# A GEGLU feed-forward kernel: ScalarE's activation table is loaded behind the last weights of the first pair

## The chip, the cores and the metric

The kernel runs on one core of a Trainium2 chip. The core has five engines with an instruction queue each: TensorE (PE, matrix products into the PSUM memory), VectorE (DVE), ScalarE (ACT), GpSimd (POOL) and SyncE (SP). Sixteen DMA engines move data between HBM and the on-chip memory SBUF. In this kernel DMAs are issued from SP's queue and from ScalarE's queue. The metric is the device time of one execution in microseconds (us); the median of several runs is compared.

## What is computed

```python
def _gelu(x):
    return jax.nn.gelu(x, approximate=True)

# x: [1, 2048, 1024], w_gate and w_up: [1024, 3584], w_down: [3584, 1024], all bfloat16
def reference(x, w_gate, w_up, w_down):
    return (_gelu(x @ w_gate) * (x @ w_up)) @ w_down
```

## The kernel before

The 2048 tokens are worked on in two halves of 1024, each half as two blocks of 512 tokens (`tb` 0 and 1). The 1024 inner rows of x and of the weights are cut into eight slices of 128 (`kd` 0 to 7; `KH` is 4, `KD` is 8). The 3584 columns of `w_gate` and `w_up` are loaded in chunks of 512, and a chunk holds two pairs of 128-column blocks. Each half first makes h = gelu(gate) * up for 14 pairs, then the product with `w_down`. Nearly all of this uses seven products in place of eight for a 2x2 scheme of blocks (Strassen's way): sums of weight blocks, called s1, s2, s3, s4 and a22, and sums of x blocks, called t1 to t4 and b22, are made beforehand by POOL, VectorE and ScalarE, and TensorE multiplies these sums in fp32r. `pair_quads` does that for a pair; its products are m1, m5, m6, m2, m7, m3 and m4. In m5 the sum s1 is used, in m6 s2.

Only the first pair of the first half is done with plain products (`first_pair_units`), since its sums could not be ready. TensorE starts with seven matmuls on constants (`warm`, L201-L211). For token block 0 the slices 0 to 3 of x come as rows (`load_x0`, two loads for the first half of the columns and one for the second) and TensorE turns them (`transpose_x0`); VectorE and, for slice 3, ScalarE (L311) copy the result from PSUM. The slices 4 to 7 and all of token block 1 are turned by DMA transposes on SP's queue (`load_xT`, L168-L175). While the first pair is multiplied, POOL makes s1, s2 and s4 of the second pair from columns 256 to 511 of the first chunk (`s_sum`, L378), and VectorE makes s3 and the t sums.

The order of the instructions on each engine is written out by hand: the helpers `sp`, `act`, `dve`, `pool` and `pe` tie each instruction to the one before it on its engine. What stands on the queues at the start is:

- ScalarE: x columns 0-255, second half of the rows (L188); x columns 256-511 (L190); gate slices 2-4 of the first 256 columns (L192); the activation table (L194); gate slices 5-7 and up slices 5-7 of the same columns (L217-L219); then the copy of L311 and the gelus.
- SP: x columns 0-255, first half of the rows; gate slices 0-1; up slices 0-1; up slices 2-4 (L187-L193); four transposes for slices 4 to 7 of token block 0 (L216); three for token block 1, of 2, 2 and 4 slices (L221); gate and up of columns 256-511 (L223); chunk 1 of gate and up, whole (L226).

Between the engines, the program's planner places the DMAs of both queues in one list, gives each a completion semaphore out of eight in turn, and lets a DMA wait until the one that used its semaphore before has landed in full. Where two queues meet in this list is worked out by the planner and is not written in the code. The instruction records of the trace show each DMA's semaphore and what it waits for.

```python
    load_w(first, 1, 2, 5, sp, 0, FA)
    act(nc.scalar.preload_act_table(ACT.Gelu_apprx_tanh))
...
    for kd in range(KH, KD):
        load_xT(xT, 0, 0, kd, kd + 1)
        if kd == KH + 1:
            for j in range(2):
                load_w(first, j, 5, KD, act, 0, FA)
```

Of the kernel before, what the change touches and what calls it, by code (L numbers as in the profile page):

```python
# [8 lines left out]
ACT = mybir.ActivationFunctionType  # L9
# [25 lines left out]
def kernel(  # L35
# [8 lines left out]
    nc = tc.nc  # L44
# [65 lines left out]
    def on(engine, inst):  # L110

        if engine in last_on:
            tc.add_manual_dep(
                inst.ins, last_on[engine].ins.name, SCHED_DEP, reason="engine order"
            )
        last_on[engine] = inst
        return inst
# [4 lines left out]
    def act(inst):  # L122
        return on("act", inst)
# [31 lines left out]
    def load_w(key, j, k0, k1, queue=sp, f0=0, f1=FG):  # L155

        c0 = key[1] * FG
        eng = nc.scalar if queue is act else nc.sync
        src = (wgv, wuv)[j][:, k0:k1, c0 + f0 : c0 + f1]
        queue(eng.dma_start(out=chunks[key][j][:, k0:k1, f0:f1], in_=src))  # L160
# [7 lines left out]
    def load_xT(xT, h, tb, k0, k1):  # L168
        t0 = h * SH + tb * TB
        sp(  # L170
            nc.sync.dma_start_transpose(
                out=xT[tb][:, k0:k1, :],
                in_=xv[t0 : t0 + TB, k0:k1, :],
            )
        )  # L175
# [15 lines left out]
    load_w(first, 1, 0, 2, sp, 0, FA)  # L191
    load_w(first, 0, 2, 5, act, 0, FA)  # L192
    load_w(first, 1, 2, 5, sp, 0, FA)  # L193
    act(nc.scalar.preload_act_table(ACT.Gelu_apprx_tanh))  # L194
    ident = const_pool.tile([P, P], BF16, name="ident")
    make_identity(nc, ident[:])

# [17 lines left out]
    for kd in range(KH, KD):  # L215
        load_xT(xT, 0, 0, kd, kd + 1)  # L216
        if kd == KH + 1:  # L217
            for j in range(2):
                load_w(first, j, 5, KD, act, 0, FA)  # L219
    for k0, k1 in ((0, 2), (2, KH), (KH, KD)):  # L220
        load_xT(xT, 0, 1, k0, k1)  # L221
    for j in range(2):
# [779 lines left out]
```

## Time and profile before

| | us |
|---|---|
| median of 7 runs | 539.99 (539.79 to 540.49) |
| the profiled execution | 540.73 |
| its span, first to last instruction | 538.7 |
| TensorE matmuls busy | 532.8 |
| VectorE, ScalarE, POOL busy | 363.5, 263.2, 244.6 |
| table load on ScalarE (L194) | 1.283, from 2.35 to 3.63 |

The profile is of one execution. Its page gives the busy time of each engine and its share of the span; then the span in 40 equal slices, each digit the busy tenths of a slice, with the clock that was granted to TensorE (PEclk); the DMA queues; the chain of work that ended last, followed back from the end; and the costliest groups of instructions. A timeline line has the start, the duration, the engine, the line of the code, the operation, what is written and read, how many instructions were merged, and in brackets how long the engine sat idle ahead of it and what ended that. "PEld" is TensorE's weight load, "ACTq" and "SPq" are the issuing of DMAs by ScalarE and SyncE. Names such as `w_mem` (weights), `s_mem` (the s sums), `t_mem` (the t sums) and `bank` (PSUM) are those of the code. A busy share of the DMA engines over 1 means that packets of one engine overlap. Some records of matmuls are missing in a trace, which shows as a gap of exactly one matmul.

### The profile page before, as it was taken

The page shows a single profiled execution, that of the slowest core. Times are in us where ns is not written, and L with a number is a line of the kernel's source. Part 1 is how long each engine was busy: PE and PEld are TensorE (multiplying, and loading weights), DVE is VectorE, ACT ScalarE, POOL GpSimd, SP SyncE. Part 2 cuts the span into 40 slices and gives each one's busy share as a digit, 9 for nine tenths or more (in the row PEclk, how much of TensorE's full clock was granted, in tenths as well). Part 3 has the DMA queues.
Part 4 walks back from the last instruction along what each step waited for, and adds up shares of the span by engine and source line. Part 5 has one row for each costly group of instructions (what it writes and reads, how often), then busy time and mean ns, then how long its engine had stood idle before and what let it go on. Part 6 is the DMA issues. An engine that isn't in the chain of part 4 may idle for free.

```text
span 538.7 us, 7067 instructions
## 1 busy us (share of the span) xinstructions
PE 532.8 (99%) x2348; PEld 378.1 (70%) x2384; DVE 363.5 (67%) x475; ACT 263.2 (49%) x446; POOL 244.6 (45%) x212
## 2 busy tenths in 40 slices
PE   9999999999999999999999999999999999999997
PEld 4577777766776676777776777777777766866866
DVE  1988776788775997889574334444444469969961
ACT  1655555555555319217465555555555551452270
POOL 0699877777776000000056776666777730000000
PEclk9999999999999999999999999999999999999999
DMA  9936776697815977789950404042222448677846
GB/s 207 318 127 199 196 262 191 213 241 237 289 63 196 359 244 244 240 271 306 329 174 1 156 1 158 16 141 66 91 78 80 157 137 284 226 242 243 293 144 208
DMA packets 92435, 102.70 MB, mean 191 GB/s; under 512 B 18672, under 2 KB 67312, under 8 KB 92400
## 3 DMA queue, kind: packets, MB, share of 16 engines
q1 hardware_dynamic: 69600, 80.30, 47.0%
q10 hardware_dynamic: 22800, 21.96, 13.1%
q8 instruction: 19, 0.31, 0.3%
q14 instruction: 16, 0.13, 0.1%
HBM read 85.98 MB, written 12.58 MB: 183 GB/s over the span
## 4 chain that ended last, share of the span: by engine, by line
PE 99%; issue 0%; ACT 0%; ACTq 0%
PE bank L406 63%; PE bank L693 33%; PE bank L257 3%; PE bank L203 1%; PE bank L301 0%; ACT o_sb L746 0%; ACT bank L461 0%; ACTq L746 0%; ACTq L461 0%
## 5 line engine op out<-in xcount | busy, mean ns | idle before, releaser
L406 PE MATMUL bank<-t_mem,s_mem 128*128 128x512 f32 x1056 | 249.6, 394 | 0.0
L406 PEld LDWEIGHTS bank<-t_mem,s_mem 128*128 128x128 f32 x1056 | 198.1, 188 | 44.1 <-DVE bank L429 0.4
L378 POOL TENSOR_TENSOR s_mem<-w_mem 128x512 fp32r<-128x512 bf16 x102 | 120.7, 1205 | 190.8 <-DMA out_dram<-o_sb 103.1
L693 PE MATMUL bank<-t_mem,s_mem 128*128 128x512 f32 x544 | 127.1, 392 | 0.0
L281 DVE TENSOR_TENSOR hT<-w_mem,bank 128x512 bf16<-128x512 f32 x104 | 71.2, 686 | 80.5 <-PE bank L406 46.2
L693 PEld LDWEIGHTS bank<-t_mem,s_mem 128*128 128x128 f32 x544 | 102.2, 188 | 22.1
L429 DVE TENSOR_TENSOR bank<-bank,m 128x512 f32<-128x512 f32 x108 | 69.9, 694 | 44.4 <-ACT m L451 43.3
L406 PE MATMUL bank<-xT,w_mem 128*128 128x512 bf16 x405 | 96.5, 380 | 1.4
L276 ACT ACTIVATE w_mem<-bank 128x512 f32<-128x512 f32 x104 | 61.8, 596 | 53.4 <-DVE bank L429 35.8
L406 PEld LDWEIGHTS <-w_mem 128*128 128x128 bf16 x432 | 40.2, 98 | 51.6 <-issue 6.8
L378 POOL TENSOR_TENSOR s_mem<-w_mem,s_mem 128x512 fp32r<-128x512 bf16 x52 | 65.9, 1293 | 0.0
L598 DVE TENSOR_TENSOR t_mem<-w_mem 128x1024 fp32r<-128x1024 bf16 x56 | 65.5, 1216 | 0.0
L378 POOL TENSOR_TENSOR s_mem<-s_mem,w_mem 128x512 fp32r<-128x512 f32 x52 | 60.7, 1189 | 0.0
L457 ACT COPY bank<-bank 128x512 f32<-128x512 f32 x54 | 30.8, 570 | 38.9 <-PE bank L406 38.9
L391 ACT CAST s_mem<-w_mem 128x512 fp32r<-128x512 bf16 x54 | 33.1, 615 | 30.6 <-PE bank L406 28.0
L668 DVE TENSOR_TENSOR s_mem<-hT 128x512 fp32r<-128x512 bf16 x52 | 34.2, 684 | 10.0 <-PE bank L693 9.4
L451 ACT COPY m<-bank 128x512 f32<-128x512 f32 x54 | 31.7, 587 | 17.5 <-PE bank L406 17.5
L693 PEld LDWEIGHTS <-hT 128*128 128x128 bf16 x224 | 21.3, 98 | 26.6 <-issue 2.1
L461 ACT COPY bank<-bank 128x512 f32<-128x512 f32 x54 | 30.7, 570 | 12.7 <-PE bank L406 12.7
L746 ACT CAST o_sb<-bank 128x512 bf16<-128x512 f32 x28 | 15.4, 586 | 39.6 <-PE bank L693 39.6
L623 DVE TENSOR_TENSOR o_sb<-wd_sb,o_sb 128x512 fp32r<-128x512 bf16 x28 | 31.5, 1125 | 0.5
L595 ACT CAST t_mem<-w_mem 128x1024 fp32r<-128x1024 bf16 x28 | 26.9, 1048 | 0.0
(42 smaller groups left out, 238.3 us busy)
## 6 DMA issues: line engine op xcount, KB each, us to landing
t_mem<-t_dram SPq DMA_DIRECT2D x56, 512.0 KB, 5.2
w_mem<-in_w_gate_dram ACTq DMA_DIRECT2D x10, 1024.0 KB, 5.2
w_mem<-in_w_up_dram ACTq DMA_DIRECT2D x10, 1024.0 KB, 5.4
wd_sb<-in_w_down_dram SPq DMA_DIRECT2D x28, 256.0 KB, 4.2
t_dram<-o_sb SPq DMA_DIRECT2D x28, 256.0 KB, 2.8
wd_sb<-in_w_down_dram SPq DMA_DIRECT2D x12, 512.0 KB, 7.8
w_mem<-in_w_down_dram SPq DMA_DIRECT2D x4, 1024.0 KB, 6.3
w_mem<-in_w_down_dram SPq DMA_DIRECT2D x8, 512.0 KB, 8.6
```

The source lines that it names most:

```text
L276: act(nc.scalar.activation(out=g_sb, in_=ps[:], func=ACT.Gelu_apprx_tanh))
L281: nc.vector.tensor_tensor(out=hT[:, fc, tb * TB : (tb + 1) * TB], in0=g_sb, in1=ps[:], op=ALU.mult,)
L378: pool(nc.gpsimd.tensor_tensor(out=t, in0=in0, in1=in1, op=op))
L391: act(nc.scalar.copy(out=t, in_=a(1, 1)))
L406: nc.tensor.matmul(banks[bank][:], lhsT=lhs[:, c, :], rhs=rhs[:, c, :], start=start and c == 0, stop=c == KH - 1, skip_group_check=True,)
L429: nc.vector.tensor_tensor(out=banks[dst][:], in0=banks[src][:], in1=m5[j][:], op=ALU.add)
L451: act(nc.scalar.copy(out=m5[j][:], in_=banks[V_[j]][:]))
L457: act(nc.scalar.copy(out=banks[RB[j]][:], in_=banks[QB[j]][:]))
L598: dve(nc.vector.tensor_tensor(out=t, in0=in0, in1=in1, op=ALU.subtract))
L623: dve(nc.vector.tensor_tensor(out=t, in0=in0, in1=in1, op=ALU.subtract))
L668: dve(nc.vector.tensor_tensor(out=t, in0=in0, in1=in1, op=op))
L693: nc.tensor.matmul(banks[bset[u]][:], lhsT=lhs(i, u), rhs=rhs(i), start=start and i == 0, stop=stop and i == NS - 1, skip_group_check=True,)
```

## The change

The load of the activation table is moved on ScalarE's queue from its place ahead of the weight slices 5 to 7 to the place behind them. No other line is changed.

```diff
@@ -191,7 +191,6 @@
     load_w(first, 1, 0, 2, sp, 0, FA)
     load_w(first, 0, 2, 5, act, 0, FA)
     load_w(first, 1, 2, 5, sp, 0, FA)
-    act(nc.scalar.preload_act_table(ACT.Gelu_apprx_tanh))
     ident = const_pool.tile([P, P], BF16, name="ident")
     make_identity(nc, ident[:])
 
@@ -217,6 +216,7 @@
         if kd == KH + 1:
             for j in range(2):
                 load_w(first, j, 5, KD, act, 0, FA)
+            act(nc.scalar.preload_act_table(ACT.Gelu_apprx_tanh))
     for k0, k1 in ((0, 2), (2, KH), (KH, KD)):
         load_xT(xT, 0, 1, k0, k1)
     for j in range(2):
```

## The prediction

> **What bounds the kernel now.** I read the page first (busy shares, slices, chain of waits), then the timeline of the first 27 us, then busy times by stretch. From the page:
>
> ```profile
> PE 532.8 (99%) x2348; PEld 378.1 (70%) x2384; DVE 363.5 (67%) x475; ACT 263.2 (49%) x446; POOL 244.6 (45%) x212
> PEclk9999999999999999999999999999999999999999
> PE 99%; issue 0%; ACT 0%; ACTq 0%
> ```
>
> TensorE is busy from 0.77 us to 535.5 us and is nearly the whole chain. A change can only save what TensorE stands still for, or make it stand still. Matmuls of 512 columns start 0.427 us apart up to about 6.5 us and 0.216 us apart from 7.06 on, with no pause up to 20 us that a missing record doesn't explain. The issuing queues, from the timelines of ScalarE and SyncE:
>
> ```profile
> 0.74 1.02 ACTq L166 DMA_DIRECT2D w_mem<-in_x_dram  x2
> 1.79 0.53 ACTq L160 DMA_DIRECT2D w_mem<-in_w_gate_dram  x1
> 2.35 1.28 ACT L194 ACT_TABLE_LOAD   x1 [2.35 <-issue]
> 5.25 0.38 ACTq L160 DMA_DIRECT2D w_mem<-in_w_gate_dram  x1
> 5.90 0.44 ACTq L160 DMA_DIRECT2D w_mem<-in_w_up_dram  x1
> 7.26 0.58 ACT L311 COPY xT<-bank 128x512 bf16<-128x512 bf16 x1 [3.63 <-PE bank L301]
> ...
> 2.77 9.84 SPq L171 DMA_TRANSPOSE xT<-in_x_dram  x7
> 12.65 1.06 SPq L160 DMA_DIRECT2D w_mem<-in_w_gate_dram  x1
> ```
>
> The table load ends at 3.63, yet ScalarE's next weight load is issued at 5.25: something else held it. The trace's instruction records name each DMA's semaphore. There are eight, dealt in turn over both queues together, and from the ninth on a DMA waits for the full landing of the one eight places ahead. The places, with landings: 1 x on ACT (3.67), 2 x on SP (3.45), 3 the second x load on ACT (5.23), 4 gate rows 0-1 (4.16), 5 up 0-1 (5.88), 6 gate 2-4 on ACT (6.56), 7 up 2-4 (6.85), 8, 9, 10 the transposes of x slices 4, 5, 6, 11 gate 5-7 on ACT, 12 the transpose of slice 7, 13 up 5-7 on ACT, 14 to 16 the three large transposes of the second token block, 17 gate columns 256-511, 18 the same of up. So late gate (11) waits for place 3, 5.23, and goes at 5.25; late up (13) waits for place 5, 5.88, and goes at 5.90.
>
> The far end of SP's queue is on the path. From 18 to 27 us:
>
> ```profile
> 18.51 4.33 POOL L378 TENSOR_TENSOR s_mem<-w_mem 128x512 fp32r<-128x512 bf16 x2 [17.21 <-DMA w_mem<-in_w_gate_dram]
> 22.81 3.19 POOL L378 TENSOR_TENSOR s_mem<-s_mem,w_mem 128x512 fp32r<-128x512 f32 x2
> ...
> 26.05 0.19 PEld L406 LDWEIGHTS bank<-t_mem,s_mem 128*128 128x128 f32 x1
> ```
>
> POOL starts when place 17 has landed (18.44), makes s1 and s2 of the second pair without a break and ends at 26.00; TensorE's load of that last s2 starts at 26.05, right behind, while the matmul ahead of it started at 26.01. From the landing of place 17 to a matmul there is no slack.
>
> **The change part by part.** The table load leaves its place between ScalarE's third and fourth DMA and comes behind the fifth. Nothing is added, and nothing is written on SP's or POOL's queue.
>
> 1. *The ACT loads.* ScalarE is free at 2.31. In the program's list the table load stood behind place 7 and ahead of the first transpose; I take late gate to stand there now, as place 8, which waits for nothing: issue near 2.35, 2.9 us earlier. Late up comes one issue later (about 0.5 us), beside the first transpose, waits for a landing of 3.45 or 3.67, and goes near 3.7. TensorE needs these rows at 10.51 and had them at 9.75, so nothing is gained by it.
> 2. *SP's transposes.* They move back by one and two places. The first gets place 9 or 10 and waits for 3.67 or 3.45 instead of going at 2.77: +0.9. The second gets place 11, and with it the wait that late gate had: the second x load, 5.23. It goes at 5.25 instead of 4.03, **+1.22 us**. The next ones wait for landings that are past by then. From the second transpose to place 17 SP took 12.65 - 4.03 = 8.62; place 17 now goes at 13.87. From there the places are as before.
> 3. *Is the landing as late as the issue?* If the DMA engines were behind, a later issue would cost nothing. By stretch (PE, PEld, DVE, ACT, POOL, clock, DMA share, GB/s):
>
> ```profile
> 9.00:10.00 1.00, 1.00 (x6) 0.49 (x5) 0.00 (x0) 0.00 (x0) 0.00 (x0) 1.00 1.27 232
> 10.50:11.00 0.50, 0.50 (x4) 0.25 (x3) 0.00 (x0) 0.00 (x0) 0.00 (x0) 1.00 0.61 140
> 14.00:14.50 0.50, 0.50 (x4) 0.26 (x3) 0.50 (x1) 0.00 (x0) 0.00 (x0) 1.00 1.28 286
> ```
>
> At 10.5 the share falls from 1.27 to 0.61: slice 7 has landed (10.44) and the first large transpose, issued at 7.92, is only beginning; at 14 the share is back at 1.28. From 10.5 on SP's issue sets the pace, and the later transposes and place 17 follow one behind another. I take the shift whole, 1.22; the other bound is nothing, if the 384 KB of late weights that now go earlier leave the engines free enough to catch up.
> 4. *Who waits.* TensorE needs the last large transpose at 16.55 and had it at 15.88: 1.22 later is 17.10, a stall of 0.55. Then s1 and s2 end 1.22 later and the load of 26.05 starts at 27.27; the 0.55 lies within that. The matmuls behind it are shifted whole, since from pair to pair TensorE is the bound (12.51 us each). VectorE's t2 starts with that transpose too (16.32) and moves by about as much as POOL; the sums for the next product, s4, had 0.70 us to spare (28.12 against 28.81) and move along. Cost +1.22.
> 5. *The table load* starts after late up, near 4.1, and ends near 5.4; the copy of 7.26 still waits for TensorE alone. Cost nothing; the cover is 1.9 us. Behind it ScalarE has nothing but that copy and, at 12.65, the first gelu.
>
> Sum: the profiled execution took 540.73 us (span 538.7, 2.03 around it), 0.74 above the median of the seven runs; 540.73 + 1.22 = 541.95 for it, and 539.99 + 1.22 = **541.2** for the median.
>
> **Rivals.** *The engines catch up.* For it: in stretches before 10.5 the share is over 1.2, and six of the seven transposes needed 3.8 to 4.8 us to land, while single ones later (99.6 us in the trace) land in 2.6, so some 1 us of each was queueing. Against: the gap at 10.5. Then 0 to 0.9 of the 1.22 is left, 540.0 to 540.9, mean 540.4. It decides as soon as 0.14 us of the shift is caught up, for a difference of 0.2% (1.08 us) is about what a measurement of this kernel can tell from no change. The same outcome comes if late up falls behind the second transpose in the list: then SP shifts by 0.92 only, 540.9. This rival ends on the other side of my forecast.
>
> *The places don't change*, since the list is dealt differently: late gate still goes at 5.25, late up at 5.90 to 6.34, the table load runs 6.35 to 7.63 and the copy 7.63 to 8.22. TensorE's first matmul on its slice is at 8.78, so by the rows it costs nothing: 540.0. The largest stall the rows allow is a second table load's length more, 8.22 + 1.28 - 8.78 = 0.72: 540.7. The Trainium skill, "ScalarE: Activation LUTs", section "What ACT_TABLE_LOAD costs", gives the load 1283 ns, which this trace shows to the nanosecond, and another 1380 ns to drain, which it can't show, since the next issue waits for a landing. By the page the copy would end near 9.6 and TensorE would stall 0.8 us, an estimate from its figure; by the row alone nothing.
>
> *It grows on the way.* The second x load lands later still because late gate shares the engines with it, or POOL's first two ops (2.24 and 2.13 us beside a busy VectorE, 1.16 to 1.62 later) fall differently against VectorE. Twice the shift is 2.4: 542.4. Against: late gate is behind the x load on the same queue.
>
> *Faster.* Weights 2.9 us earlier could free the engines for the transposes, and place 17 would land earlier. But TensorE waits only 0.04 us for it; a gain of over 1.08 us would need stalls that the chain doesn't show. At most 0.1: 539.9.
>
> **How the numbers follow.** Full shift 0.58, of which 0.45 above the bound and 0.13 below it (541.2 is close to it); engines catch up or a smaller shift 0.16; places unchanged 0.11; grows 0.11; faster 0.04, half of that too small to matter. Slower by over 0.2%: 0.45 + 0.11 = 0.56. Within: 0.13 + 0.16 + 0.11, and from the last case 0.02, 0.42. Faster 0.02. The range goes from 540.0 (places unchanged or all caught up) to 542.0 (full shift and half of its growth); outside are some 0.04 below and 0.08 above. The full shift's own range is 540.9 to 541.7.
>
> **What would show it.** Late gate issued near 2.35 and late up near 3.7, with the table load behind them by 5.5; the second transpose at 5.25 behind the second x load; place 17 at 13.9; POOL's first op near 19.7, not 18.51; TensorE's pause before the load of 26.05, now near 27.3; the span 1.2 us longer and TensorE's busy time the same. I am wrong if SP's transposes keep their times, if place 17 still lands near 18.4, or if the copy at 7.26 is late.

## The result, and the profile after

The changed kernel's median is 541.22 us (540.73 to 542.14, 13 runs) against 539.99 us (539.48 to 540.58, 31 runs): a ratio of 1.0024, 95% interval 1.0017 to 1.0031. That is 1.23 us more; 541.2 was forecast. The profiled execution took 541.22 us with a span of 539.4, 0.7 longer than that of before (538.7). Why it is 0.7 there and 1.2 in the medians is told further below.

The busy shares and the chain's shares, from the page of after:

```profile
PE 532.8 (99%) x2348; PEld 377.4 (70%) x2384; DVE 363.6 (67%) x475; ACT 263.1 (49%) x446; POOL 244.4 (45%) x212
PE 93%; DMA 2%; SPq 1%; POOL 1%; issue 1%; DVE 0%; ACT 0%; ACTq 0%
```

TensorE works exactly as long as before, 532.8 us. What is new is that 6% of the chain now lies outside TensorE, so it stood still somewhere. The timelines of ScalarE's queue and of SyncE's show the start (start, duration, engine, line, operation):

```profile
1.79 1.07 ACTq L160 DMA_DIRECT2D w_mem<-in_w_gate_dram  x2
3.79 0.37 ACTq L160 DMA_DIRECT2D w_mem<-in_w_up_dram  x1
4.19 1.28 ACT L219 ACT_TABLE_LOAD   x1 [4.19 <-DMA w_mem<-in_x_dram]
6.49 0.59 ACT L311 COPY xT<-bank 128x512 bf16<-128x512 bf16 x1 [1.01 <-PE bank L301]
...
4.04 9.60 SPq L171 DMA_TRANSPOSE xT<-in_x_dram  x7
13.68 0.58 SPq L160 DMA_DIRECT2D w_mem<-in_w_gate_dram  x1
```

Late gate is the second DMA of the first line; the records have its issue at 2.35. Late up goes at 3.79 and the table is loaded from 4.19 to 5.47, which ends 1.0 us before the copy of L311 starts at 6.49. That copy and the first gelu come earlier than in before (6.49 for 7.26, 11.97 for 12.65). SP's first transpose goes at 4.04 instead of 2.77, the second, by the instruction records, at 5.33 behind the second x load (landed 5.31), and place 17 goes at 13.68 instead of 12.65.

From place 17 on, the timeline of POOL and the chain of waits, pieces up to 31.7 us:

```profile
19.43 4.12 POOL L378 TENSOR_TENSOR s_mem<-w_mem 128x512 fp32r<-128x512 bf16 x2 [18.12 <-DMA w_mem<-in_w_gate_dram]
23.51 3.19 POOL L378 TENSOR_TENSOR s_mem<-s_mem,w_mem 128x512 fp32r<-128x512 f32 x2
```

```profile
13.68 5.67 DMA w_mem<-in_w_gate_dram
...
19.43 7.28 POOL s_mem L378 x4
...
28.59 0.04 DVE bank L429
...
29.20 1.85 DVE t_mem L252
31.04 0.62 DVE bank L429
...
31.70 3.20 PE bank L406 x13
```

Place 17 landed at 19.35 (18.44 before), POOL started 0.92 later and its fourth sum ended at 26.70 (26.00). Read alone, these lines say what the prediction said: place 17, then POOL, then TensorE. But the chain goes on through VectorE to 31.70, and POOL made up 0.22 of its 0.92 on the way. Both points turned out to matter. VectorE in the same stretch, first of after:

```profile
14.68 1.22 DVE L252 TENSOR_TENSOR t_mem<-xT,xT 128x1024 fp32r<-128x1024 bf16 x1 [0.46 <-DMA xT<-in_x_dram]
15.83 1.28 DVE L281 TENSOR_TENSOR hT<-w_mem,bank 128x512 bf16<-128x512 f32 x2
17.02 2.28 DVE L252 TENSOR_TENSOR t_mem<-xT,t_mem 128x2048 fp32r<-128x2048 bf16 x1
19.23 1.22 DVE L252 TENSOR_TENSOR t_mem<-xT 128x1024 fp32r<-128x1024 bf16 x1
...
28.59 0.70 DVE L429 TENSOR_TENSOR bank<-bank,m 128x512 f32<-128x512 f32 x1 [0.20 <-ACT bank L457]
29.20 1.85 DVE L252 TENSOR_TENSOR t_mem<-xT,t_mem 128x1024 fp32r<-128x1024 bf16 x1
30.96 1.28 DVE L429 TENSOR_TENSOR bank<-bank,m 128x512 f32<-128x512 f32 x2
```

and of before:

```profile
13.98 1.23 DVE L252 TENSOR_TENSOR t_mem<-xT,xT 128x1024 fp32r<-128x1024 bf16 x1 [0.76 <-DMA xT<-in_x_dram]
...
18.52 1.22 DVE L252 TENSOR_TENSOR t_mem<-xT 128x1024 fp32r<-128x1024 bf16 x1
...
30.25 1.28 DVE L429 TENSOR_TENSOR bank<-bank,m 128x512 f32<-128x512 f32 x2
```

The first line of each is the second half of t1 ("t1b" from here). It waits for the second large transpose, place 15, and from there VectorE works through to 32 us with one wait of 0.20. Its lines are some 0.70 later in after (two of them 0.62), t1b as well as the last, and the last matmul of the program is 0.70 later too (535.77 against 535.07). So there are two ways in which SP's delay could reach TensorE: by place 17 and POOL, or by place 15 and VectorE. SP moved both places alike, so these two profiles cannot tell them apart.

### The profile page after: what moved, and what is told of

Read it like the earlier page. It is cut to its first block, busy times and chain, and to the rows that moved or that the text cites. A ratio compares the mean times of both kernels' runs of the same rounds, so it can differ in the third digit from the quotient of the medians.

```text
span 539.4 us, 7070 instructions
## 1 busy us (share of the span) xinstructions
PE 532.8 (99%) x2348; PEld 377.4 (70%) x2384; DVE 363.6 (67%) x475; ACT 263.1 (49%) x446; POOL 244.4 (45%) x212
## 4 chain that ended last, share of the span: by engine, by line
PE 93%; DMA 2%; SPq 1%; POOL 1%; issue 1%; DVE 0%; ACT 0%; ACTq 0%
PE bank L406 61%; PE bank L693 33%; SPq L171 1%; POOL s_mem L378 1%; DMA w_mem<-in_w_gate_dram 1%; DMA w_mem<-in_x_dram 1%; DVE t_mem L252 0%; DVE bank L429 0%; ACT o_sb L746 0%; ACT bank L461 0%; ACT bank L457 0%; ACTq L166 0%; ACTq L746 0%; ACTq L461 0%
## 5 line engine op out<-in xcount | busy, mean ns | idle before, releaser
L281 DVE TENSOR_TENSOR hT<-w_mem,bank 128x512 bf16<-128x512 f32 x104 | 71.1, 686 | 80.1 <-PE bank L406 45.6
L451 ACT COPY m<-bank 128x512 f32<-128x512 f32 x54 | 31.7, 587 | 17.5 <-PE bank L406 17.5
```

The source lines that it names most:

```text
L281: nc.vector.tensor_tensor(out=hT[:, fc, tb * TB : (tb + 1) * TB], in0=g_sb, in1=ps[:], op=ALU.mult,)
L451: act(nc.scalar.copy(out=m5[j][:], in_=banks[V_[j]][:]))
```

## The experiments

The theory to begin with was the prediction's: the table load itself costs nothing; moving it lets late gate and late up take earlier turns among the eight semaphores, the second transpose inherits a wait for the second x load, all of SP's queue moves by some 1.2 us, and the shift goes on whole. The rivals were the table load's own cost, the earlier weights crowding out the transposes, and the engines catching up; later, VectorE's way against POOL's.

In the diffs, `behind(a, b)` makes the planner list a behind b, which sets its turn among the semaphores and adds no wait; with `SYNC_DEP` it is a real wait. Medians are compared with before on the same chip (540.29 in the first group, 540.26 in the second, 540.13 in the third).

| kernel | t1b starts | place 17 issued | last matmul less t1b | median | less before | ratio (95%) |
|---|---|---|---|---|---|---|
| before | 13.98 | 12.65 | 521.08 | 539.99 | | |
| after | 14.68 | 13.68 | 521.08 | 541.22 | +1.23 | 1.0024 (1.0017 to 1.0031) |
| e1 places back | 13.28 | 12.81 | 521.27 | 540.37 | +0.08 | 1.0004 (0.9995 to 1.0013) |
| e3 places moved | 14.23 | 13.59 | 521.10 | 541.30 | +1.01 | 1.0021 (1.0012 to 1.0029) |
| e4 between | 13.56 | 12.85 | 521.13 | 540.63 | +0.34 | 1.0003 (0.9995 to 1.0012) |
| e5 wait for x | 15.66 | 15.01 | 521.09 | 542.67 | +2.41 | 1.0045 (1.0032 to 1.0058) |
| e6 two slices | 14.28 | 14.05 | 521.21 | 540.75 | +0.49 | 1.0006 (0.9997 to 1.0014) |
| e7 only place 17 | 13.03 | 12.99 | 521.34 | 540.38 | +0.09 | 1.0003 (0.9994 to 1.0012) |
| f1 late place 17 | 13.96 | 14.78 | 521.22 | 540.62 | +0.49 | 1.0012 (1.0003 to 1.0021) |
| f2 late t1b | 15.38 | 12.84 | 521.19 | 542.07 | +1.94 | 1.0036 (1.0023 to 1.0049) |
| f3 products first | 14.35 | 12.88 | 520.00 | 539.92 | -0.21 | 0.9996 (0.9987 to 1.0005) |
| f4 sums free | 14.49 | 13.67 | 521.08 | 541.25 | +1.12 | 1.0020 (1.0011 to 1.0029) |

The second to fourth columns come from one profiled execution each, the medians from all timed ones; the ratio is formed within rounds, so it is not the quotient of the two medians to the last digit. A step of 0.001 in the ratio is 0.54 us.

**e1: after, with the turns put back.** On the changed kernel:

```diff
+    tr = [load_xT(xT, 0, 0, kd, kd + 1) for kd in range(KH, KH + 3)]
+    late = behind(load_w(first, 0, 5, KD, act, 0, FA), tr[2])
+    tr.append(behind(load_xT(xT, 0, 0, KD - 1, KD), late))
+    behind(load_w(first, 1, 5, KD, act, 0, FA), tr[3])
+    act(nc.scalar.preload_act_table(ACT.Gelu_apprx_tanh))
```

> The changed kernel, with the DMAs put back into the order of the kernel before in the planner's list (the two late weight loads are tied behind the third and the fourth transpose), the table load still behind them. Theory (the transposes inherit waits on semaphores): the second transpose goes at 4.0 us again, place 17 at 12.6, and the time is 540.0, the time of the kernel before, within 0.4. Rival, the table load's new place costs (it runs from 6.35 to 7.63, and the copy of 7.26 is late): 540.7. Rival, weights that come earlier crowd the DMA engines: here they come late again, so 540.0 too; this run doesn't tell it from the theory.

The second transpose went at 4.02 again and place 17 at 12.81; the median is that of before. The timeline of ScalarE of e1, and a line of TensorE's:

```profile
1.79 4.09 ACTq L164 DMA_DIRECT2D w_mem<-in_w_gate_dram  x2
6.25 0.37 ACTq L164 DMA_DIRECT2D w_mem<-in_w_up_dram  x1
6.66 1.28 ACT L222 ACT_TABLE_LOAD   x1 [6.66 <-DMA w_mem<-in_w_up_dram]
7.95 0.58 ACT L314 COPY xT<-bank 128x512 bf16<-128x512 bf16 x1
```

```profile
8.59 1.24 PE L260 MATMUL bank<-xT,w_mem 128*128 128x512 bf16 x5 [0.41 <-ACT xT L314]
```

Here the table load runs right up to the copy of L314 (L311 of before) and delays it, and TensorE stands still behind that copy. Even so the time is that of before, within an interval from 0.3 us less to 0.7 more. With e3 below: the turns cost, and for the table's place no cost can be measured. The Trainium skill ("ScalarE: Activation LUTs", section "What ACT_TABLE_LOAD costs") adds 1380 ns of drain to the 1283 ns of the load. These rows don't show it: the copy starts at 7.95, within 0.01 of the load's end.

**e3: before, with the turns of after.** The table stays ahead of the late weights:

```diff
+    late = load_w(first, 0, 5, KD, act, 0, FA)
+    tr = [behind(load_xT(xT, 0, 0, KH, KH + 1), late)]
+    late = behind(load_w(first, 1, 5, KD, act, 0, FA), tr[0])
+    for kd in range(KH + 1, KD):
+        tr.append(behind(load_xT(xT, 0, 0, kd, kd + 1), late))
```

> The kernel before, its table load where it was, ahead of the late weight loads, but with the DMAs in the order of the changed kernel (gate 5-7, first transpose, up 5-7, second transpose). Theory: the second transpose goes at 5.25, place 17 at 13.7 to 13.9, POOL's first sum starts 0.9 to 1.2 later, and the time is that of the changed kernel, 541.2 within 0.4, though the table load was never moved. Rival, the table load's place: 540.0. Rival, crowding by weights at 2.35: gate goes at 3.65 here, so about half of it, 540.6.

The loss is there without the change, 1.01 us. From the timelines of ScalarE and SyncE of e3:

```profile
2.35 1.28 ACT L198 ACT_TABLE_LOAD   x1 [2.35 <-issue]
2.38 0.48 ACTq L164 DMA_DIRECT2D w_mem<-in_w_gate_dram  x1
3.66 0.38 ACTq L164 DMA_DIRECT2D w_mem<-in_w_up_dram  x1
...
3.90 9.64 SPq L175 DMA_TRANSPOSE xT<-in_x_dram  x7
13.59 0.58 SPq L164 DMA_DIRECT2D w_mem<-in_w_gate_dram  x1
```

A side finding stands in the first two lines: late gate is issued while the table loads. The load didn't keep that DMA waiting. So the kernel before didn't lose anything by having the load in that place: late gate waited for a landing.

**e4: after, with late gate and late up taking their turns between the second and the third transpose.** The weights go earlier than in before, if not as early as in after, and the wait for the second x load falls on another DMA, late up.

```diff
+    tr = [load_xT(xT, 0, 0, kd, kd + 1) for kd in range(KH, KH + 2)]
+    for j in range(2):
+        late = behind(load_w(first, j, 5, KD, act, 0, FA), tr[1])
+    act(nc.scalar.preload_act_table(ACT.Gelu_apprx_tanh))
+    for kd in range(KH + 2, KD):
+        behind(load_xT(xT, 0, 0, kd, kd + 1), late)
```

> The changed kernel with the late weight loads tied behind the second transpose and ahead of the third: they wait for places 2 and 3 and the transposes for 1, 4 and 5, which are past. Theory: gate goes at 3.5 to 4.0, up at 5.3, both earlier than in the kernel before, the transposes go at 2.8, 4.0, 5.3, 6.6 as before, and the time is 540.0 within 0.4. Rival, crowding: part of the loss stays, 540.4 to 540.9. Rival, table load: up's issue ends near 5.7, the table load near 7.0, so nothing, 540.0.

Late gate went at 3.61, late up at 5.25, the transposes at 2.76, 4.02, 5.31 and 6.62, place 17 at 12.85. The interval takes in no change and stays below after's. Late gate was 1.6 us and late up 0.7 us earlier than in before, and place 17 was issued only 0.2 later: where the wait isn't inherited, earlier weights cost little or nothing. Weights as early as after's were not tried without the wait. But place 15 landed 3.7 to 4.0 us after its issue in the four profiles with after's turns (after, e3, e8, f4) and 3.6 to 4.6 us in the seven where its turn is as in before, so the earlier weights didn't slow it.

**e5: before, with the first transpose waiting for the second x load,** so that all of SP's queue goes 2.4 to 2.6 later:

```diff
-    load_x0(1, act)
+    x1 = load_x0(1, act)
...
-        load_xT(xT, 0, 0, kd, kd + 1)
+        tr = load_xT(xT, 0, 0, kd, kd + 1)
+        if kd == KH:
+            behind(tr, x1, SYNC_DEP)
```

> The kernel before, its list of DMAs kept but for one step, with a wait more: the first transpose waits for the second x load (5.23), so all seven transposes go about 2.5 us later (the second at 6.5 instead of 4.03) and place 17 at 15.1. Theory (SP's issue sets the pace, nothing is caught up): 2.5 us more, 542.5, a slope of one. Rival (the DMA engines catch up): 541.0 to 541.8.

Late gate moved too, to 3.65 from 5.25, and by e4 that costs little. Place 17 went 2.36 later and the time grew by 2.41: one to one, though the interval spans 1.7 to 3.1. Most of the delay is not caught up, and it doesn't double.

**e6: before, with x slices 4 to 7 turned by two transposes of two slices,** meant to bring SP's queue forward:

```diff
-    for kd in range(KH, KD):
-        load_xT(xT, 0, 0, kd, kd + 1)
-        if kd == KH + 1:
+    for kd in range(KH, KD, 2):
+        load_xT(xT, 0, 0, kd, kd + 2)
+        if kd == KH + 2:
```

> The kernel before, with slices 4 to 7 transposed by two DMAs of two slices each in place of four of one, which takes two issues of 1.26 us from SP's queue ahead of place 17. Theory: place 17 goes near 10.1 instead of 12.65 and lands 1 to 2 us earlier, POOL's sums have slack, and TensorE gains what it waited: 0.04 us by the profile of before, up to 0.7 where its clock rises earlier: 539.3 to 540.0. Rival (the landing is bound by the engines' bandwidth): 540.0 to 540.3.

A miss. The five transposes now took SP 1.57, 3.02, 1.64, 2.19 and 2.63 us to issue, and place 17 went at 14.05, later than in after. It was issued 1.40 later than in before and landed only 0.37 later, at 18.81, and the time is 0.49 longer, within the bound. The transpose that answers to place 15 was late as well (14.16), so the run doesn't part the two ways.

**e7: before, with place 17 alone made to wait** for the landing of the second large transpose:

```diff
-    for k0, k1 in ((0, 2), (2, KH), (KH, KD)):
-        load_xT(xT, 0, 1, k0, k1)
+    tr = [load_xT(xT, 0, 1, k0, k1) for k0, k1 in ((0, 2), (2, KH), (KH, KD))]
...
+            behind(late, tr[1], SYNC_DEP)
```

> The kernel before, with one wait more: the load of gate columns 256-511 (place 17) waits for the landing of the second large transpose (13.86 before), so it goes 1.2 us later, while all seven transposes keep their times. Theory (the loss comes through POOL's sums, which start with this landing): the time grows by what the landing is later, between 0.5 us (if the data still queue behind the third large transpose) and 1.2 us: 540.5 to 541.2, and TensorE's pause is ahead of the load that waits for POOL's s2, at 26.05 before. Rival, the late transposes are what costs in the changed kernel: they are on time here, so 540.0.

It did not do what it was meant to. The transpose landed at 12.91 in this execution, so place 17 went only 0.34 later than in before, and it landed at 17.38. Nothing follows for the question. But the trace shows something else, by one line of POOL's timeline and one of VectorE's:

```profile
17.45 1.22 POOL L383 TENSOR_TENSOR s_mem<-w_mem 128x512 fp32r<-128x512 bf16 x1 [16.14 <-DMA w_mem<-in_w_gate_dram]
```

```profile
17.57 2.18 DVE L257 TENSOR_TENSOR t_mem<-xT 128x1024 fp32r<-128x1024 bf16 x1
```

POOL began 0.12 ahead of VectorE here, and its sum took 1.22, while VectorE's took 2.18. In before and after VectorE began first or together; its sum took 1.22 and POOL's took 2.24 (18.51 to 20.75) and 2.02 (19.43 to 21.45). One engine stands still while the other finishes. The Trainium skill ("SBUF — State Buffer", section "SBUF: two separate sides") calls the port pair that VectorE and GpSimd share an exclusive lock, held for the whole instruction by the one that starts first; among the VectorE instructions that contend for it the page names those with two inputs in SBUF, and this sum is one. These rows agree. It follows that POOL's end can be VectorE's doing. In eleven profiles (before, after, e1, e3, e4, e5, e6, e8, e9, f1 and f4) POOL's first sum ended 6.76 to 6.77 us after t1b began, although POOL itself started anywhere from 18.08 to 20.34. Where POOL began ahead of that sum of VectorE's (e7, f2), and where t1b itself was put later (f3), it was 5.63 to 5.69.

**e8 and e9: after and before, with m5, m6 and m3 of the second pair reading the sum s1 of gate in place of s1, s2 and s4,** so that TensorE waits for less of POOL:

```diff
+            if (h, pair) == (0, 1) and name in ("s1", "s2", "s4"):
+                return ssum[(0, 1, 0, "s1")]
```

> The changed kernel, but the products m5, m6 and m3 of the second pair all read the first sum that POOL makes (s1 of gate) in place of s1, s2 and s4, so TensorE doesn't wait for POOL's chain there. POOL still makes all sums; the output is wrong for this pair. Theory (the loss comes through POOL's sums): 540.0 to 540.4. Rival (the loss comes through the late transposes and through VectorE, whose t sums start with them; the pauses near 12.5, 16.5 and 20.7 us): still 541.2. A part of each: between them.

> The same release from POOL's chain in the kernel before, as the base for the run beside it. In the profile of before TensorE waited 0.04 us for that chain, so by theory 539.9 to 540.3; where the clock of TensorE rises earlier, POOL's chain binds more, and it could be down to 539.5.

Both came out far slower, 545.36 and 544.25, for a reason of their own. POOL writes the third pair's sum into the buffer of s1 ahead of m3, so m3 now had to wait for that sum, and TensorE stood 3.0 us for POOL. Behind this standstill the granted clock was 0.50 from 32.5 to 35.5 us in both profiles, and TensorE's matmuls came 0.43 us apart in place of 0.23. From TensorE's weight loads of e9:

```profile
30.93 3.26 PEld L406 LDWEIGHTS bank<-t_mem,s_mem 128*128 128x128 f32 x11 [3.05 <-POOL s_mem L378]
```

The design was at fault, and the two runs say nothing on the question. f4 repeats it without m3.

**f1: before, with three small loads ahead of place 17,** which hold up place 17 and nothing ahead of it:

```diff
+    pad = const_pool.tile([P, 3 * 64], BF16, name="pad")
+    for i in range(3):
+        cols = slice(i * 64, (i + 1) * 64)
+        sp(nc.sync.dma_start(out=pad[:, cols], in_=x2[0:P, cols]))
```

> The kernel before with three small loads of 16 KB into an unread tile put on SP's queue between the last large transpose and place 17, so that places 17 and 18 go about 1.3 us later, while all seven transposes keep their times. The theory of the prediction (no slack from the landing of place 17 through POOL's sums): 0.7 to 1.3 us more, 541.0 to 541.5. The new theory: VectorE is the path. In the runs so far POOL's first sum ends 6.77 us after VectorE's second t1 piece starts, whenever POOL started, and TensorE's last matmul starts 521.1 us after that piece; it waits for the second large transpose (place 15). Then POOL may start 0.8 us later without harm: 540.0 to 540.5.

Place 17 went 2.13 later and landed only 0.24 later (18.68): 3.90 us after its issue, against 5.79 in before. The result, +0.49, lies between the two forecasts. Place 15 landed late in this execution too, at 13.84, so the test is weak.

**f2: before, with t1b alone made to wait** for the third large transpose. No DMA is touched:

```diff
+    tr1 = [load_xT(xT, 0, 1, k0, k1) for k0, k1 in ((0, 2), (2, KH), (KH, KD))]
...
-        t_sum("t1", KH // 2, KH)
+        behind(t_sum("t1", KH // 2, KH), tr1[2], SYNC_DEP)
```

> The kernel before, no DMA touched: VectorE's second t1 piece is made to wait for the third large transpose (15.1 to 15.9) instead of the second (12.9 to 13.9). New theory (everything VectorE does up to 31 us follows this piece without a break): 1.2 to 2.0 us more, the last matmul 521.1 us behind the start of the piece: 541.5 to 542.2. The prediction's theory (place 17 and POOL decide, VectorE has slack): 540.0 to 540.5.

Place 17 landed at 18.23, even earlier than in before, and POOL started at 18.30; yet the time grew by 1.94. From VectorE's timeline of f2:

```profile
15.38 1.23 DVE L256 TENSOR_TENSOR t_mem<-xT,xT 128x1024 fp32r<-128x1024 bf16 x1 [2.33 <-DMA xT<-in_x_dram]
...
31.72 1.28 DVE L434 TENSOR_TENSOR bank<-bank,m 128x512 f32<-128x512 f32 x2
```

Place 15 landed at 13.32 in this execution, and in before t1b starts 0.12 behind that landing; without the added wait it would have started at 13.44. By this estimate the edit held it up by 1.94, and the time grew by 1.94 (the interval allows 1.2 to 2.6). POOL was not left untouched: it and VectorE held each other up, and its fourth sum ended at 26.80 (26.00 in before). But TensorE didn't wait for it. The waits of its matmuls in f2 between 7 and 36 us, and the last one of its weight loads (total, times, longest):

```profile
PE bank L411 <- ACT bank L466: 1.3, 1, 1.3
PE bank L411 <- DVE bank L434: 0.3, 1, 0.3
...
PEld bank L411 <- DVE bank L434: 0.6, 1, 0.6
```

The copy of L466 is ScalarE's, and it had waited 1.7 us for a product of VectorE's (L286). So all three are VectorE's, and no line of TensorE's waits names POOL. This is the decisive run: with place 17 early, a delay of t1b goes one to one into the time by VectorE's way.

**f4: after, with m5 and m6 alone reading s1,** so that TensorE no longer waits for POOL's last sums at 26.70:

```diff
+            if (h, pair) == (0, 1) and name in ("s1", "s2"):
+                return ssum[(0, 1, 0, "s1")]
```

> The changed kernel; in the second pair m5 and m6 all read the first sum that POOL makes (s1 of gate) in place of s1 and s2 of both, so TensorE doesn't wait there for POOL's chain (m3 reads its own s4 again, unlike the earlier run, where it read a sum that had been overwritten for the third pair and waited for that). The output is wrong for this pair. The prediction's theory: back to 540.0 to 540.5. New theory: VectorE holds TensorE a little later, at m4; it waits some 0.2 us for a copy that follows m6, so 540.9 to 541.3.

The time stays that of after, 541.25. TensorE's pause for POOL is gone, and the one for VectorE is left. From VectorE's timeline of f4 and from TensorE's weight loads:

```profile
14.49 1.23 DVE L252 TENSOR_TENSOR t_mem<-xT,xT 128x1024 fp32r<-128x1024 bf16 x1 [0.47 <-DMA xT<-in_x_dram]
...
30.77 1.28 DVE L431 TENSOR_TENSOR bank<-bank,m 128x512 f32<-128x512 f32 x2
```

```profile
31.50 1.46 PEld L406 LDWEIGHTS bank<-t_mem,s_mem 128*128 128x128 f32 x7 [0.52 <-DVE bank L431]
```

**f3: before, with VectorE's two products of L281 ahead of t1b,** so that it works while it waits for place 15:

```diff
-        t_sum("t1", KH // 2, KH)
         ...
+        t_sum("t1", KH // 2, KH)
```

> The kernel before with VectorE's two multiplications of the first block (0.68 us each, ready at 13.3 and 13.7) put ahead of the second t1 piece, so that they fill its wait for the transpose. New theory: VectorE's t2 then waits for the third large transpose alone and goes up to 0.4 us earlier; where VectorE binds, 0.2 to 0.4 us less, 539.7 to 540.2. The prediction's theory: 540.0 to 540.5, no change.

The difference of 0.21 us can't be told from nothing. The two products take 1.2 us, t1b then starts only at 14.35, and with place 15 near its mean landing (13.35, below) little is left to win. No kernel of the study beats before measurably.

## Why the prediction was right, and where it was not

*Step 1, the ACT loads: right.* Late gate 2.35 as said, late up 3.79 for 3.7.

*Step 2, SP's transposes: right.* The second transpose went at 5.33 (5.25 said), place 17 at 13.68 (13.87 said). The first went 1.27 later instead of 0.9, because the first x load on ScalarE's queue landed at 4.03 and not 3.67; the second transpose's wait covers that. e3 has this step without the change, e1 the change without this step, and e4 the early weights without the inherited wait: the loss is there in the first alone.

*Step 3, the landing is as late as the issue: right for SP's queue as a whole.* In e5 place 17 is issued 2.36 later and the time is 2.41 longer. The rival "the engines catch up" falls with e5, and so does "it grows". For place 17 by itself the step doesn't hold: in f1 it went 2.13 later and landed 0.24 later. The gap in the DMA share that the step argued from was thin as well: the half microsecond behind the 0.61 had a share of 1.79.

*Step 4, who waits: wrong in its path.* The sentence was "From the landing of place 17 to a matmul there is no slack". What carries the delay is place 15: it lands, t1b starts, and VectorE then goes through sixteen instructions, t1b among them, with one wait of 0.2, to the addition that TensorE's m4 waits for. That VectorE's t2 "moves by about as much as POOL" was written there as a side matter; it was the path, and t2 came late behind t1b and not, as written there, with the last large transpose. f2 delays t1b alone and costs 1.94; f4 takes TensorE's waits for s1 and s2 away and saves nothing. TensorE's load right behind POOL's end, the row the step rested on, is real, but POOL's first sum ends when VectorE lets it, 6.77 us after t1b in eleven profiles. The stall of 0.55 that the step put at the last large transpose was some 0.2 there (landed at 16.57, the matmul at 16.61), and one of 0.5 came at the first, which the step had not named (place 14 landed at 12.90, the matmul at 12.94). The size survived because SP moves places 15 and 17 together; that the number came out right is luck as far as this step goes. The trace of before had the row that I should have weighed, the last pause of TensorE's weight loads between 7 and 36 us (total, times, longest):

```profile
PEld bank L406 <- DVE bank L429: 0.4, 1, 0.4
```

TensorE already stood waiting for VectorE there, behind POOL's sums, and f4 shows that the wait that came last decided.

*Step 5, the table load costs nothing: right.* It had 1.0 us to spare in after (load ended 5.47, copy at 6.49, when TensorE was ready). In e1 it had none, the copy came late, TensorE waited 0.41 us for it, and the time still did not grow measurably. The rival "the places don't change" fell with the places, which did change.

*The sum.* 539.99 + 1.22 = 541.2 against 541.22. In the profiled pair only 0.70 shows, where the sum forecast 541.95 for that execution. In these two place 15 landed 0.70 apart, at 13.86 and 14.56. What the change moves is its issue: 9.27 or 9.28 where its turn is as in before (9.52 in f1), 10.40 to 10.54 with the turns of after, so 1.1 to 1.3 later. Its landing spreads more. With the turn of before it came at 13.86 (before), 13.16 (e1), 12.91 (e7), 13.12 (e9), 13.84 (f1), 13.32 (f2) and 13.23 (f3), a mean of 13.35; with the turns of after at 14.56 (after), 14.11 (e3), 14.40 (e8) and 14.37 (f4), a mean of 14.36. The difference of the means is 1.01, against a measured 1.23. The profiled execution of before had a late landing, and that is part of why it stood 0.74 above its median, but not the larger part: TensorE lost only some 0.2 us to VectorE there (matmuls at 30.65, 30.99 and 31.33, which are 0.23 apart elsewhere). Its matmuls also went over from 0.427 to 0.216 us apart later than in any other profile, at 6.7 us. In e7 that was at 5.8, and the same matmul that starts at 7.06 in before starts at 6.63 there.

*What stays open.* Neither e7 nor f1 made place 17 land much later while place 15 stayed, so how much room POOL's way has by itself was not measured. In the profiles with an early place 15 (e1, e7) the last matmul comes 521.27 and 521.34 after t1b instead of 521.08, and TensorE's waits between 9 and 36 us name neither VectorE nor POOL. There its own matmuls bind, and a still earlier place 15 would win nothing. How often that is so in the other executions is not known.

## What to carry to other kernels

Where DMAs of several queues take completion semaphores in turn, moving any instruction on one queue can hand a wait to another: list the turns, and ask which DMA inherits which landing. A chain of waits names the last releaser, not the engine that stretched it; where two engines hold each other up, look for the instruction whose distance to the end stays nearly the same from profile to profile. And when one cause moves two candidate paths alike, the right size proves neither of them: delay each by itself.

## What the runs showed of the hardware

- VectorE and POOL hold each other up for whole instructions. The same POOL sum took 1.22 us when it began first (e7) and 2.24 when it began together with VectorE's (before); the same VectorE sum 1.22 and 2.18.
- A table load on ScalarE and a DMA issue on its queue go side by side (e3: load 2.35 to 3.63, issue at 2.38), and a copy on ScalarE follows the load within 0.01 us (e1 and e4).
- Fewer, larger transposes didn't make SP's queue shorter: in e6 the first two of two slices took 1.57 and 3.02 us to issue, where one slice takes 1.2 to 1.3. Size alone doesn't set it, for the two-slice transposes of before, at 7.92 and 9.27, took 1.30 each. Why the early ones took longer was not tested.
- A later issue can land nearly as early: place 17 issued 2.13 later landed 0.24 later (f1), 1.40 later landed 0.37 later (e6). That less lay ahead of it in the DMA engines is a likely reason, not a tested one.
- The step of TensorE's matmuls from 0.427 to 0.216 us apart came between 3.5 and 6.7 us after the start, at another moment in each profiled execution (4.9 in after, 6.7 in before). After a standstill of 3.0 us TensorE went back to 0.43 us for some 3.4 us (e8 and e9).
